# Keys of strided heads kept in order of time, and read with a step by the score products

## The chip, the cores and the metric

The kernel runs on one core of a Trainium2 chip. The metric is the device time of one execution in microseconds (us). The core's engines are TensorE (PE in the rows; PEld is its weight load), VectorE (DVE), ScalarE (ACT), GpSimd (POOL) and SyncE (SP), which issues the DMAs here.

## The reference

Three layers follow each other. The first is attention with 4 batches, 8 heads, 576 tokens and 64 values a head; four heads are local (a query sees the last 32 tokens), four are strided (a query sees the earlier tokens whose number has the same remainder by 32). The second is a layer with a softmax-weighted unit and a layer norm, the third a product of two projections.

```
scores = scale * np.matmul(q, k.transpose(0, 1, 3, 2))
mask_local = (rel >= 0) & (rel < stride)                                    # heads 0 to 3
mask_strided = (rel >= 0) & (pos[None, :] % stride == pos[:, None] % stride)   # heads 4 to 7
scores = np.where(masks, scores, -1e9);  attn = softmax(scores);  attn_out = attn @ v
h = x @ w_in;  solu = h * softmax(h);  ln = (solu - mu) / np.sqrt(var + 1e-06) * g_ln;  x = ln @ w_out
out = (x @ w_a) * (x @ w_b) @ w_out2
```

Inputs and outputs are float32; the weights arrive in 64-bit form and are converted in the kernel.

## The kernel before, in words

Attention works on pairs of heads: four pairs in each of four batches, two local and two strided. For each pair the queries and keys of 576 tokens are loaded in fp32 (rawq, rawk), transposed on TensorE into a PSUM tile s (line 594, six transposes each), and evacuated by ScalarE into qkT, queries in qkT[:, 0], keys in qkT[:, 1], so that the head dimension lies on partitions and the tokens along the free axis.

For a strided pair, two neighbouring tokens share a row of the load, so that partitions 0 to 63 hold the even tokens and 64 to 127 the odd ones. The columns that come out of the transpose are in order of time: for each head 18 periods t of 16 residues a. The evacuation (line 602) writes them by residue, h a t, so that the 18 tokens of a residue lie side by side: it reads PSUM in order and writes with a step of 18 fp32 words. For local pairs the evacuation is plain (line 605). The time that the planner is told for these is in line 606.

A strided tile (two for each pair, one for the even and one for the odd residues) covers 16 residues of two heads in twelve cells. A cell takes the queries of up to three residues, 54 columns, as the stationary operand and the keys of the same residues, 54 columns, as the moving one (lines 677 to 680); the cells of the sixth run have one residue, 18 columns. Before the cells a product of an identity with a mask fills the PSUM tile (line 676). In the trace each fp32 product is two records. Then follow the row maximum and softmax on VectorE and ScalarE (lines 692 to 710), the transposing of the probabilities (on TensorE in batch 0, line 739; by DMA afterwards, line 763), and the products with V (line 773 in batch 0, lines 778 to 780 afterwards), and ScalarE puts the output into xT (line 800). The layer after it takes tiles of 128 tokens (line 831, matmuls with w_in; line 881, with w_out) and runs among the attention of later batches. The third layer follows (lines 1268 and 1333).

The order of all instructions is set by a planner. Each step tells its engine and how long it should take; the planner makes a list schedule of them, then 40 more with keys that are taken from the schedule backward and shifted at random (fixed seed), and keeps the shortest. A changed time of one step can therefore move instructions of every engine anywhere in the program. Loads and stores go through SyncE's queue in the planned order, and a load stands there until its buffer is free.

Of the kernel before, what the change touches and what calls it, by code (L numbers as in the profile page):

```python
# [19 lines left out]
B, H, S, D = 4, 8, 576, 64  # L20
# [6 lines left out]
NR = S // ST  # L27
RP = ST // 2
# [222 lines left out]
def tile_banded_attention_solu_bilinear(  # L251
# [13 lines left out]
    nc = tc.nc  # L265
# [5 lines left out]
    def pe(us, fn, r, w, cols=60): return P.op("PE", us, fn, r, w, cols)  # L271
    def dve(us, fn, r, w): return P.op("DVE", us, fn, r, w)
    def act(us, fn, r, w): return P.op("ACT", us, fn, r, w)
# [253 lines left out]
    for b in range(B):  # L527
        for pr in range(H // 2):
            g = groups[b][pr] = Group()
# [55 lines left out]
    def group_T(g):  # L585
        g.T = rings["qkT"].new()
        for c in range(2):
            tp = rings["s"].new()
            raw = g.raw[c]

            def transposes(tp=tp, raw=raw):
                for m in range(NM):
                    i, o = divmod(m, NM // 2)
                    nc.tensor.transpose(tp()[:, i, QT * o:QT * o + QT], raw()[:, m].rearrange("p h d -> p (h d)"),  # L594
                                        ident[:QT, :QT])
            pe(NM * 0.085, transposes, ((raw, 0), (raw, 1), "ident"), (tp,), NM * 72)

            def evac(c=c, tp=tp):
                src = tp()[:, :, :S // 2]
                dst, sc = g.T()[:, c], 1.0 if c else D ** -0.5  # L600
                if g.strided:
                    nc.scalar.activation(dst.rearrange("p (h a t) -> p h t a", h=2, t=NR),  # L602
                                         src.rearrange("p h (t a) -> p h t a", t=NR), AF.Copy, scale=sc)
                else:
                    nc.scalar.activation(dst.rearrange("p (i t) -> p i t", i=2), src, AF.Copy, scale=sc)
            act(1.2 if g.strided else 0.66, evac, (tp,), ((g.T, c),))

    def vdims(g):
        return (128, len(RUNS) * 2 * D) if g.strided else (KB, NB * 2 * D)
# [31 lines left out]
    def att_tile(g, j, fine):  # L641
# [28 lines left out]
        def scores():  # L670
            s = sp()
            last = {(c[1], c[3]): n for n, c in enumerate(cells)}
            for f in banks:
                for rows, stop in ([(slice(0, 128), False)] if len(last) == 2 * len(banks) else
                                   [(slice(64 * x, 64 * x + 64), (f, x) not in last) for x in range(2)]):
                    nc.tensor.matmul(s[rows, f, :npb * nk], identb[:, rows], mask[:, :npb], start=True, stop=stop)  # L676
            for n, (h, f, col, half, _, nq, q0, kk, k0, *_) in enumerate(cells):
                w = slice(64 * f, 64 * f + 64)
                nc.tensor.matmul(s[64 * half:64 * half + nq, f, col:col + kk], g.T()[w, 0, q0:q0 + nq],  # L679
                                 g.T()[w, 1, k0:k0 + kk], start=False, stop=n == last[f, half])  # L680
        pe(ng * nk * 0.42e-3 + sum(0.04 if c[3] else 4 * c[7] / 2.4e3 for c in cells) + 0.03, scores,
           ((g.T, 0), (g.T, 1), "identb", "masks" if g.strided else "maskl"), (sp,),
           ng * nk + sum(c[7] for c in cells))
# [103 lines left out]
        t0 = g.b * S % XR  # L787
# [153 lines left out]
    def attention(b):  # L941
        P.sooner = pm["sooner"]
        gs = order[4 * b:4 * b + 4]
        ts = batch_tiles(b)
        P.key = pm["att"] * b - pm["pre"]
        for p in (gs[:2], gs[2:]):
            for g in p:
                load_v(g)
            if b not in pm["direct"]:
                pair_scale(p)  # L950
        for n, (g, j) in enumerate(ts):
            P.key = pm["att"] * (b + n / len(ts))
            if not j:
                P.key -= pm["pre"]
                group_T(g)
                if b not in pm["direct"]:
                    group_v(g)
                load_next()
                P.key += pm["pre"]
            att_tile(g, j, (b * len(ts) + n) in pm["fine"])  # L960
        P.sooner = 0.0
# [402 lines left out]
    for ps in range(NP):  # L1364
        for i in range(NSB):
            n = (i + ps) % NSB
# [67 lines left out]
```

## Time and profile before

| | |
|---|---|
| median of three timed runs | 757.65 us (756.41 to 758.9) |
| profiled execution | 755.28 us |
| its span, first to last instruction | 752.9 us |
| TensorE busy | 727.9 us, 97% |
| mean granted TensorE clock | 0.983 of full speed |

The span is cut by the profile into work of the engines and idle time; each idle stretch is put down to the event that ended it. A busy TensorE counts records from start to end, and records overlap, so how long a group of products takes is best read from the start of one group to the start of the next. The granted clock is 1.00 at 2.4 GHz and 0.5 at 1.2 GHz; a value between them is a stretch with both.

### The profile page before, as it was taken

What the parts mean: (1) busy time and instruction counts of PE and PEld (TensorE: products, weight loads), DVE (VectorE), ACT (ScalarE), POOL (GpSimd) and SP (SyncE); (2) the same over time, 40 slices, a digit from 0 to 9 for tenths busy, and PEclk for the clock granted to TensorE, in tenths of its full rate; (3) what the DMA queues carried; (4) which work ended last, traced back from release to release, by engine and by line L of the source; (5) the groups of instructions that cost most, each with busy time, mean ns of one, the idle gap of its engine ahead of it and who ended that gap; (6) DMA issues with size and microseconds to landing.
All of it is one profiled execution on the core that took longest, in us unless ns stands there. A gap on an engine that the chain in (4) does not pass through costs nothing.

```text
span 752.9 us, 14306 instructions
## 1 busy us (share of the span) xinstructions
PE 727.9 (97%) x5564; PEld 484.5 (64%) x5564; DVE 524.6 (70%) x1020; ACT 430.2 (57%) x800; POOL 119.9 (16%) x194
## 2 busy tenths in 40 slices
PE   6989899999999998989999999999999999999997
PEld 4867677878787786877645655556555545555553
DVE  5799988857757775898799998737777463435253
ACT  4568887676677677885666766537263433133130
POOL 4352436232513432210000000000000000000000
PEclk9989799999999999999999999999999999999999
DMA  9779997979874864976536234315614131720405
GB/s 209 187 174 234 195 177 164 255 148 190 146 132 91 184 138 93 246 184 240 169 118 244 66 112 141 113 57 175 221 43 129 57 104 40 228 85 30 139 1 167
DMA packets 156963, 109.59 MB, mean 146 GB/s; under 512 B 101344, under 2 KB 135136, under 8 KB 156896
## 3 DMA queue, kind: packets, MB, share of 16 engines
q1 hardware_dynamic: 156896, 108.69, 56.1%
q8 instruction: 43, 0.70, 0.4%
q14 instruction: 24, 0.20, 0.1%
HBM read 65.41 MB, written 27.53 MB: 123 GB/s over the span
## 4 chain that ended last, share of the span: by engine, by line
PE 90%; DVE 5%; ACT 2%; DMA 1%; issue 1%; POOL 0%; POOLq 0%; SPq 0%; DVEq 0%; ACTq 0%
PE M L1268 32%; PE o L1333 18%; PE h L831 14%; PE y L881 12%; PE s L679 4%; PE s L594 3%; PE xbank L778 2%; PE xbank L773 1%; PE s L676 1%; PE xbank L780 1%; PE xbank L779 1%; ACT qkT L602 1%; DMA rawk<-in_k_dram 1%; DMA lnT<-ln 1%; PE Q L897 0%
## 5 line engine op out<-in xcount | busy, mean ns | idle before, releaser
L1268 PE MATMUL M<-y,w 128*128 128x384 f16 x1512 | 258.1, 326 | 1.4 <-DVE y L1215 1.3
L1268 PEld LDWEIGHTS <-w 128*128 128x128 f16 x1512 | 147.0, 98 | 101.8 <-issue 2.1
L1333 PE MATMUL o<-wo,p 128*128 128x512 f16 x648 | 148.4, 379 | 0.2 <-DVE p L1320 0.2
L1333 PEld LDWEIGHTS <-p 128*128 128x128 f16 x648 | 63.1, 98 | 71.1 <-DVE p L1320 0.7
L881 PE MATMUL y<-lnT,wout 128*128 128x256 f16 x864 | 102.7, 274 | 3.0 <-ACT ys L884 1.9
L881 PEld LDWEIGHTS <-wout 128*128 128x128 f16 x864 | 82.7, 98 | 17.4 <-issue 4.8
L831 PE MATMUL h<-win,xh 128*128 128x512 f32 x288 | 81.1, 423 | 0.7 <-DVE wk L840 0.6
L1275 ACT COPY M<-M 128x384 f32<-128x384 f32 x72 | 33.6, 467 | 57.8 <-PE M L1268 57.6
L831 PEld LDWEIGHTS h<-win,xh 128*128 128x128 f32 x288 | 55.4, 200 | 12.6 <-DVE wk L840 1.0
L1318 ACT ACTIVATE p<-A 128x384 f16<-128x384 f32 x72 | 36.9, 522 | 37.3 <-DVE A L1317 37.0
L1340 DVE SCALAR_TENSOR_TENSOR ob<-o,osc,op 128x512 f32<-128x512 f32 x36 | 27.0, 749 | 41.0 <-PE o L1333 31.3
L1279 DVE TENSOR_TENSOR A<-M,V 128x384 f32<-128x384 f32 x36 | 19.8, 555 | 40.3 <-PE M L1268 40.3
L1290 ACT COPY V<-M 128x384 f32<-128x384 f32 x36 | 17.2, 477 | 46.7 <-PE M L1268 46.5
L1320 DVE SCALAR_TENSOR_TENSOR p<-A,p 128x384 f16<-128x384 f32 x72 | 39.0, 552 | 6.1 <-ACT p L1318 5.1
L831 PE MATMUL h<-win,xl 128*128 128x512 f32 x144 | 41.5, 412 | 0.0
L679 PE MATMUL s<-qkT 64*54 64x54 f32 (+2 forms) x672 | 38.7, 257 | 2.7 <-ACT qkT L602 2.7
L445 DVE SCALAR_TENSOR_TENSOR f64f<-f64f,raw 128x512 int32<-128x512 int32 x52 | 39.2, 758 | 1.8 <-ACT f64f L438 1.1
L438 ACT ACTIVATE f64f<-raw 128x512 f32<-128x512 f32 x52 | 34.1, 667 | 6.0 <-DMA raw<-in_moe_w_b_dram 3.7
L1317 DVE TENSOR_TENSOR A<-A,M 128x384 f32<-128x384 f32 x36 | 19.9, 552 | 24.5 <-PE M L1268 24.4
L679 PEld LDWEIGHTS s<-qkT 64*54 64x54 f32 (+2 forms) x672 | 28.1, 146 | 13.4 <-issue 4.6
L692 DVE TENSOR_REDUCE mx<-s 128x6 f32<-128x324 f32 (+2 forms) x40 | 19.2, 485 | 20.8 <-PE s L679 20.8
L861 DVE SCALAR_TENSOR_TENSOR ln<-wk,st,ln 128x1024 f16<-128x1024 f32 x18 | 24.4, 1358 | 13.0 <-ACT ln L860 13.0
(170 smaller groups left out, 1156.9 us busy)
## 6 DMA issues: line engine op xcount, KB each, us to landing
raw<-in_moe_w_out_dram SPq DMA_DIRECT2D x20, 512.0 KB
o_scr<-ob SPq DMA_DIRECT2D x36, 256.0 KB
op<-o_scr SPq DMA_DIRECT2D x36, 256.0 KB
raw<-in_moe_w_a_dram SPq DMA_DIRECT2D x12, 512.0 KB
raw<-in_moe_w_b_dram SPq DMA_DIRECT2D x12, 512.0 KB
y_scr<-y SPq DMA_DIRECT2D x14, 384.0 KB
y<-y_scr SPq DMA_DIRECT2D x14, 384.0 KB
y_scr<-ys SPq DMA_DIRECT2D x18, 256.0 KB
```

The costliest lines, as they stand in the source:

```text
L438: act(0.67, lambda: nc.scalar.activation(f(), raw()[:, :, 1].bitcast(F32), AF.Copy, scale=2.0 ** -112), (raw,), (f,))
L445: nc.vector.scalar_tensor_tensor(fi, fi, 3, raw()[:, :, 0], op0=ALU.logical_shift_left, op1=ALU.bitwise_or)
L679: nc.tensor.matmul(s[64 * half:64 * half + nq, f, col:col + kk], g.T()[w, 0, q0:q0 + nq], g.T()[w, 1, k0:k0 + kk], start=False, stop=n == ...
L831: nc.tensor.matmul(h()[:, 512 * n:512 * n + 512], xs[xa]()[:, kk], win[wa][:, kk, 512 * n:512 * n + 512], start=(pi == 0 and kk == 0), sto ...
L861: dve(1.29, lambda: nc.vector.scalar_tensor_tensor(ln()[:, 1], e(), st()[:, 7:8], ln()[:, 0], op0=ALU.mult, op1=ALU.subtract), (e, (st, 7) ...
L881: nc.tensor.matmul(y()[:, 256 * mi:256 * mi + 256], wout[:, kk, wa, 128 * m:128 * m + 128], lnT()[:, xa, kk], start=(pi == 0 and kk == 0), ...
L1268: nc.tensor.matmul(bank()[:, :HB], w()[:, wa, a, kk], y7[b]()[:, xa, kk], start=first and pi == 0 and kk == 0, stop=pi == 2 and kk == 1, s ...
L1275: act(TA, lambda: nc.scalar.copy(dst()[:, :HB], src()[:, :HB]), (src,), (dst,))
L1318: act(TA, lambda x=x, v=v: nc.scalar.activation(v(0), x(), AF.Copy, scale=2.0 ** -PEXP), (x,), ((pu, 0, c, t),))
L1320: dve(TD, lambda x=x, v=v: nc.vector.scalar_tensor_tensor(v(1), x(), 2.0 ** -PEXP, v(0), op0=ALU.mult, op1=ALU.subtract), (x, (pu, 0, c, t ...
L1333: nc.tensor.matmul(o(), pus[u]()[:, xa, c, 128 * tt:128 * tt + 128], wo()[:, 2 * u + c, wa], start=(u == 0 and c == 0 and pi == 0), stop=( ...
L1340: dve(0.75, lambda: nc.vector.scalar_tensor_tensor(ob(), o(), osc()[:, tt:tt + 1], op(), op0=ALU.mult, op1=ALU.add), (o, osc, op), (ob,))
```

## The change

Only the queries of a strided pair are still written by residue. Its keys are evacuated as those of local pairs are, in order of time, and the score products pick a residue's keys with an access pattern: up to three residues, one word apart, by 18 periods, 16 words (64 bytes) apart. The planner is told 0.66 us for this evacuation instead of 1.2 us. Queries, masks, probabilities and V keep their layout, and the columns of a cell come in the same order as before.

```diff
             def evac(c=c, tp=tp):
                 src = tp()[:, :, :S // 2]
                 dst, sc = g.T()[:, c], 1.0 if c else D ** -0.5
-                if g.strided:
+                if g.strided and not c:
                     nc.scalar.activation(dst.rearrange("p (h a t) -> p h t a", h=2, t=NR),
                                          src.rearrange("p h (t a) -> p h t a", t=NR), AF.Copy, scale=sc)
                 else:
                     nc.scalar.activation(dst.rearrange("p (i t) -> p i t", i=2), src, AF.Copy, scale=sc)
-            act(1.2 if g.strided else 0.66, evac, (tp,), ((g.T, c),))
+            act(1.2 if g.strided and not c else 0.66, evac, (tp,), ((g.T, c),))
...
+            def tokens(c, f, t0, n):
+                t = g.T()[64 * f:64 * f + 64, c]
+                if not (g.strided and c):
+                    return t[:, t0:t0 + n]
+
+                h, a = divmod(t0 // NR, RP)
+                return t[:, S // 2 * h:S // 2 * h + S // 2].rearrange("p (t a) -> p a t", a=RP)[:, a:a + n // NR]
             for n, (h, f, col, half, _, nq, q0, kk, k0, *_) in enumerate(cells):
-                w = slice(64 * f, 64 * f + 64)
-                nc.tensor.matmul(s[64 * half:64 * half + nq, f, col:col + kk], g.T()[w, 0, q0:q0 + nq],
-                                 g.T()[w, 1, k0:k0 + kk], start=False, stop=n == last[f, half])
+                nc.tensor.matmul(s[64 * half:64 * half + nq, f, col:col + kk], tokens(0, f, q0, nq), tokens(1, f, k0, kk),
+                                 start=False, stop=n == last[f, half])
```

From line 686 on, a line has a number higher by 7 than before; the score products of line 679 are those of line 686.

SyncE's queue before, from the last load of the second strided pair's keys on (raws_109 is the buffer of V of the first strided pair, a raw with a number a piece of weights):

```order
L544 DMA rawk<-in_k_dram 96x6x128
L561 DMA raws_109<-in_v_dram 18x6x128
L561 DMA raws_109<-in_v_dram 18x5x128
L550 DMA rawq<-in_q_dram 96x6x64 x2
L550 DMA rawk<-in_k_dram 96x6x64 x2
L433 DMA raw_239<-in_moe_w_in_dram 128x1024
L561 DMA raws_109<-in_v_dram 18x6x128
L561 DMA raws_109<-in_v_dram 18x5x128 x3
L433 DMA raw_276<-in_moe_w_in_dram 128x1024
L433 DMA raw_287<-in_moe_w_in_dram 128x1024
L550 DMA rawq<-in_q_dram 96x6x64 x2
```

The same queue from the same load on after the change:

```order
L544 DMA rawk<-in_k_dram 96x6x128
L433 DMA raw_176<-in_moe_w_in_dram 128x1024
L550 DMA rawq<-in_q_dram 96x6x64 x2
L550 DMA rawk<-in_k_dram 96x6x64
L561 DMA raws_109<-in_v_dram 18x6x128
L550 DMA rawk<-in_k_dram 96x6x64
L433 DMA raw_256<-in_moe_w_in_dram 128x1024
L550 DMA rawq<-in_q_dram 96x6x64
L561 DMA raws_109<-in_v_dram 18x5x128 x3
L561 DMA raws_109<-in_v_dram 18x6x128
L561 DMA raws_109<-in_v_dram 18x5x128
L433 DMA raw_318<-in_moe_w_in_dram 128x1024
```

The first load of w_in now stands ahead of all loads of V, and a load of queries of the second local pair stands ahead of five of the first pair's six loads of V.

ScalarE before, from its first evacuation on (e is the probabilities before they are normed, sm their sums):

```order
L602 ACTIVATE qkT<-s 128x2x18x16 x2
L704 ACTIVATE e<-e 128x324
L709 ACTIVATE sm_253<-sm_253 128x6
L602 ACTIVATE qkT<-s 128x2x18x16
L704 ACTIVATE e<-e 128x324
L438 ACTIVATE f64f<-raw_239 128x512
L602 ACTIVATE qkT<-s 128x2x18x16
```

The same engine from the same place on after the change:

```order
L602 ACTIVATE qkT<-s 128x2x18x16
L605 ACTIVATE qkT<-s 128x576
L438 ACTIVATE f64f<-raw_176 128x512
L711 ACTIVATE e<-e 128x324
L602 ACTIVATE qkT<-s 128x2x18x16
L716 ACTIVATE sm_262<-sm_262 128x6
L711 ACTIVATE e<-e 128x324
L466 CAST win_106<-f64f 128x512
L605 ACTIVATE qkT<-s 128x576
```

The keys' evacuations are those of line 605 now, and the first conversion of w_in stands ahead of the first exponential.

TensorE before, from the fourth score tile on (line 739 transposes probabilities, line 773 is the product with V):

```order
L679 MATMUL s<-qkT 54x54 x8
L773 MATMUL xbank<-PT,raws_109 64x54
L773 MATMUL xbank<-PT,raws_109 64x18
L773 MATMUL xbank<-PT,raws_109 64x54
L773 MATMUL xbank<-PT,raws_109 64x18
L773 MATMUL xbank<-PT,raws_109 64x54 x8
L739 MATMUL y<-ident,lnT 128x128 x3
L594 MATMUL s<-ident,rawq 128x96 x6
```

TensorE from the same tile on after the change:

```order
L686 MATMUL s<-qkT 54x54 x8
L746 MATMUL y<-ident,lnT 128x128 x3
L780 MATMUL xbank<-PT,raws_109 64x54
L780 MATMUL xbank<-PT,raws_109 64x18
L780 MATMUL xbank<-PT,raws_109 64x54
L780 MATMUL xbank<-PT,raws_109 64x18
L780 MATMUL xbank<-PT,raws_109 64x54 x8
L594 MATMUL s<-ident,rawq 128x96 x6
```

The transposes of the second tile's probabilities have moved ahead of the first tile's products with V.

## Rows read from the trace of the kernel before

**Rows 1.** The page's first part: busy us, share of the span, instructions.

```profile
PE 727.9 (97%) x5564; PEld 484.5 (64%) x5564; DVE 524.6 (70%) x1020; ACT 430.2 (57%) x800; POOL 119.9 (16%) x194
```

**Rows 2.** Five stretches: length, busy us of each engine, granted clock, DMA share, GB/s.

```profile
0.00:50.00 50.00, 41.51 (x390) 32.31 (x390) 34.35 (x68) 27.09 (x53) 21.64 (x40) 0.99 0.86 190
50.00:100.00 50.00, 45.20 (x370) 34.21 (x369) 46.67 (x91) 43.03 (x86) 18.45 (x26) 0.84 0.94 204
100.00:300.00 200.00, 195.81 (x2169) 157.55 (x2170) 141.27 (x264) 143.46 (x258) 71.50 (x117) 0.99 0.75 156
300.00:400.00 100.00, 96.38 (x658) 68.14 (x655) 88.82 (x172) 70.28 (x118) 8.36 (x13) 0.98 0.63 191
400.00:753.00 353.00, 348.98 (x1987) 192.30 (x1984) 213.48 (x428) 146.37 (x289) 0.00 (x0) 1.00 0.35 112
```

**Rows 3.** Waits of TensorE: us in total, times, longest us.

```profile
PE s L679 <- ACT qkT L602: 2.7, 3, 1.6
```

**Rows 4.** TensorE in order of time: start, us, line, count, idle time before and releaser.

```profile
8.22 2.04 PE L679 MATMUL s<-qkT 64*54 64x54 f32 x24 [0.77 <-ACT qkT L602]
10.20 0.45 PE L676 MATMUL s<-masks,identb 128*128 128x324 bf16 x1
...
17.51 2.04 PE L679 MATMUL s<-qkT 64*54 64x54 f32 x24 [0.37 <-ACT qkT L602]
...
74.06 1.36 PE L679 MATMUL s<-qkT 64*54 64x54 f32 x24 [1.60 <-ACT qkT L602]
```

**Rows 5.** ScalarE's groups to 300 us: count, busy us, mean ns, idle before.

```profile
L602 ACT ACTIVATE qkT<-s 128x576 f32<-128x576 f32 x16 | 18.9, 1180 | 9.0 <-PE s L594 9.0
L605 ACT ACTIVATE qkT<-s 128x576 f32<-128x576 f32 x16 | 10.3, 651 | 5.3 <-PE s L594 5.3
```

**Rows 6.** TensorE's groups to 420 us, strided score products by shape.

```profile
L679 PE MATMUL s<-qkT 64*54 64x54 f32 x320 | 22.6, 247 | 2.7 <-ACT qkT L602 2.7
L679 PE MATMUL s<-qkT 64*18 64x18 f32 x64 | 7.1, 187 | 0.0
```

**Rows 7.** TensorE in order of time, a warm strided tile of batch 2.

```profile
142.21 1.36 PE L679 MATMUL s<-qkT 64*54 64x54 f32 x24
143.50 0.31 PE L676 MATMUL s<-masks,identb 128*128 128x324 bf16 x1
```

**Rows 8.** TensorE in order of time, matmuls of the second layer at two clocks.

```profile
52.06 3.71 PE L831 MATMUL h<-win,xh 128*128 128x512 f32 x8
55.61 1.10 PE L831 MATMUL h<-win,xl 128*128 128x512 f32 x4
...
137.76 1.98 PE L831 MATMUL h<-win,xh 128*128 128x512 f32 x8
139.57 1.07 PE L831 MATMUL h<-win,xl 128*128 128x512 f32 x4
```

**Rows 9.** Stretches of 4 us, columns as in Rows 2.

```profile
48.00:52.00 4.00, 2.48 (x28) 2.11 (x24) 3.90 (x10) 2.44 (x8) 1.36 (x1) 0.59 0.63 134
52.00:56.00 4.00, 4.00 (x13) 3.19 (x12) 3.63 (x7) 4.00 (x8) 3.44 (x3) 0.55 0.79 221
```

**Rows 10.** ScalarE's groups to 300 us, attention outputs of batch 0 by shape.

```profile
L800 ACT ACTIVATE xT<-xbank 128x288 f32<-128x288 f32 x4 | 2.8, 688 | 5.0 <-PE xbank L773 5.0
...
L800 ACT ACTIVATE xT<-xbank 128x256 f32<-128x256 f32 x4 | 1.5, 372 | 0.0
...
L800 ACT ACTIVATE xT<-xbank 128x64 f32<-128x64 f32 x2 | 0.4, 214 | 0.0
```

**Rows 11.** SyncE's queue in order of time: start, us of issuing, line, count.

```profile
2.81 0.97 SPq L561 DMA_DIRECT2D raws<-in_v_dram  x2
...
9.00 1.47 SPq L561 DMA_DIRECT2D raws<-in_v_dram  x4
...
13.81 0.88 SPq L550 DMA_DIRECT2D rawq<-in_q_dram  x2
```

**Rows 12.** TensorE in order of time, the first product with V.

```profile
21.35 0.35 PE L773 MATMUL xbank<-PT,raws 54*64 54x54 f32 x1
```

## The prediction

> **What bounds the kernel now.** I read the share of each engine first. TensorE is busy for 97% of the span; no other engine is above 70% [rows 1]. By stretches the picture is sharper [rows 2]: TensorE stands idle 8.5 us in the first 50 us, 4.8 us in the next 50, 4.2 us in the 200 us after that, and 3.6 and 4.0 us in the rest. From 100 to 300 us, where most of the attention of batches 1 to 3 runs beside the second layer's matmuls, it is 98% busy, so there any nanosecond added to TensorE's stream lengthens the run and any taken off ScalarE alone gives nothing. Only in the first 100 us does another engine end waits of TensorE often enough to matter.
>
> The next view is the time that TensorE waits, by what ends it. For an evacuation of transposed queries or keys of a strided pair it waits 2.7 us before score products, in three places [rows 3]: 0.77 us at 8.22, 0.37 us at 17.51 and 1.60 us at 74.06 [rows 4]. Each time the evacuation that ends the wait is that of the keys: the transposes of rawk come last before it.
>
> **The evacuations.** Eight groups (two strided pairs in each of four batches) evacuate queries and keys. The strided form takes 1180 ns each, sixteen times; the plain form for the same 576 columns takes 651 ns [rows 5]. The change turns the eight of the keys into the plain form: 8 x 0.53 = 4.2 us less on ScalarE. Of that only what lies ahead of a waiting TensorE counts: at most 0.53 us in each of the three waits, so 0.53 + 0.37 + 0.53 = 1.4 us. The other five are hidden behind matmuls already, as no wait stands there. The ends for this term are 0 (whatever conversion stands next on ScalarE takes the place) and 4.2 us (all eight count). I take 1.4 us, because the waits are rows, not a guess.
>
> **The score products.** Nothing is added in number: a strided tile still issues 12 products in 24 records, and in a tile 20 records have 54 key columns and 4 have 18: 320 and 64 in sixteen tiles [rows 6]. What changes is how the keys are read: before, 54 neighbouring fp32 words; now three runs of 18 words, each word 64 bytes from the next. No row of the trace shows TensorE reading a stepped moving operand, so this is bounded from both sides.
>
> First, what a record costs now. Between two mask products the 24 records of a warm tile fill 142.21 to 143.50, that is 1.29 us or 54 ns each [rows 7]. In the first 20 us the same tile takes 8.22 to 10.20, 1.98 us or 82 ns each [rows 4]; the granted clock reads 1.00 there too, but the second layer's products that later take 226 ns (1.81 us for eight) take 464 ns (3.71 us for eight) in the stretch where it reads 0.55 [rows 8, 9], so I read the early tiles as run at the lower level, 1.2 GHz, too. Four tiles (batch 0) are of that kind, twelve are warm. That record also tells the rate at which TensorE takes an fp32 word: 512 columns in 226 ns, 0.44 ns a column, which is one column per cycle at 2.4 GHz. So 54 ns is about 22 ns of weight load, 22 ns of key columns and some 10 ns besides; it is a sum, since all products of a tile use the same 64 rows of the array. A slower key stream therefore adds to the record in full.
>
> Second, what a step does elsewhere in this kernel. ScalarE writes the stepped evacuation at 72 bytes from word to word. Against the plain form it loses (1180 - 651) / 576 = 0.92 ns a word. Its plain rate is (372 - 214) / (256 - 64) = 0.82 ns a word, from two unstepped outputs of line 800; the stepped output of the same line, 288 words 128 bytes apart, comes to (688 - 161) / 288 = 1.83 ns, with the 161 ns of fixed time that the two unstepped rows leave [rows 10]. So a step of this size halves the rate: 0.82 to 1.74 or 1.83 ns.
>
> The Trainium skill ("SBUF — State Buffer", section "SBUF: two separate sides") has a rule that speaks against the change: SBUF is read in lines of 16 bytes, and a stream that does not hit a line at least twice pays for each new one. With 64 bytes from word to word every key would be on a line of its own. The two ScalarE rows agree with it for writes; for a read by TensorE no row does, and the page gives no size.
>
> The ends are then these. Below: zero, if TensorE fetches ahead or reads each word in one go whatever its neighbours are; a gain is excluded, because the columns stay the same in number. Above: the whole stepped word time of ScalarE, 1.74 ns. A 54-column record would gain 54 x (1.74 - 0.42) = 71 ns, an 18-column record 24 ns; a warm tile 20 x 71 + 4 x 24 = 1.52 us, twelve of them 18.3 us; a tile at the lower level 54 x (1.74 - 0.83) = 49 ns in a record, 1.05 us a tile, four of them 4.2 us; in all 22.5 us. Between the ends I take the factor that the ScalarE rows show, not their time: a rate halved from 0.42 to 0.83 ns a word. A 54-column record gains 22.5 ns and an 18-column record 7.5 ns, a warm tile 20 x 22.5 + 4 x 7.5 = 0.48 us, twelve 5.8 us. At the lower level a column takes 0.83 ns already, so the four early tiles gain nothing. All twelve warm tiles lie in stretches where TensorE does not wait, with the exception of the one at 74.06, so I count the 5.8 us in full. What comes late behind a longer tile is the row maximum on VectorE, which waits for it, and behind that the softmax chain; TensorE has products of the second layer to run meanwhile, so I add nothing for these.
>
> **The order.** The planner is given 0.66 us in place of 1.2 us for eight evacuations and lays out the whole program anew, on all five engines. Two places deserve a price. On SyncE's queue the first load of w_in now stands ahead of all loads of V, and five of the six loads of the first pair's V stand behind a load of queries that must wait until the second pair's query transposes have freed the buffer; before, all six were ahead of it. That load was issued at 13.81 us and an issue takes 0.37 to 0.49 us, so the last of V is asked for by about 16.5 us, and the first product that reads it stood at 21.35 us [rows 11, 12]: almost 5 us to land. On ScalarE the first conversion of w_in now stands ahead of the first exponentials. If its data came late, the softmax of the first tile would stand behind it; the conversion is 0.67 us. On TensorE a block of probability transposes moves ahead of the first products with V, which gives those loads 0.8 us more. I charge nothing for the order and put 3.5 us to either side, about what the idle time of TensorE between 100 and 300 us could shrink or grow by.
>
> **Sum.** 5.8 - 1.4 = +4.4 us against the profiled execution, which took 755.28 us (a span of 752.9 us and 2.4 us around it): 759.7 us. That execution lies 2.4 us under the median of the three timed runs, 757.65 us, so on the scale of the median the forecast is 762 us.
>
> **Rivals.** (1) The step is free for TensorE. For it: the port takes one word per cycle of its own whatever the array does with it, and nothing in the trace shows TensorE's reads held up. Against it: ScalarE's rows. Only the gain is left: 757.65 - 1.4 = 756.2 us, with the order's 3.5 us to each side, so 752.7 to 759.7. This is the case that ends on the other side. (2) A new line costs TensorE the same time as it costs ScalarE, 1.74 ns a word, not the same factor. For it: if the time is that of the memory and not of the engine, this is what would be seen, and the Trainium skill's rule as worded would allow it. Against it: ScalarE pays for writes, and TensorE only reads. 757.65 + 22.5 - 1.4 = 778.7 us. (3) The order decides: the new layout meets a wait that the planner does not see, for instance the first exponentials behind a late w_in, or a different fall of the granted clock in 48 to 56 us, where it reads 0.59 and 0.55 [rows 9]. With a step that is free, one more 4 us stretch at the lower level in a TensorE-bound part would cost up to 2 us, so this would end near 759 to 761 us. It is a part of the spread of the other cases rather than a case with its own hardware cause.
>
> **How the numbers follow.** I give 0.42 to the forecast, 0.37 to a free step (the order's spread included) and 0.21 to the full word time. About 0.3% of this time, 2.3 us, is what a measurement of this kernel can tell from no change. Of the free case a bit over half is faster than 755.4, the rest mostly the same, a little slower: 0.19, 0.12, 0.06. Of the forecast's case 0.05 is faster and 0.08 the same, by the order's luck. The third is slower outright. That makes 0.24 faster, 0.20 the same and 0.56 slower. The forecast alone spans 758 to 766; the range that should hold 8 in 10 goes from 753, the low end of the free case, to 778, which takes in about half of the costly one.
>
> **What would show it.** The score tiles decide: a warm tile that still takes 1.29 us means a free step, about 1.8 us means halving, about 2.8 us the full word time. The eight evacuations of keys should read about 650 ns beside eight at 1180, and the waits of TensorE for them shrink from 2.7 to about 1.3 us. If the tiles are unchanged and the run is still slower, the order is the cause, and TensorE's idle time or its granted clock before 350 us must show it. If TensorE's busy time grows by 5 us and the span does not, then TensorE was not the bound I took it for.

## The result, and the profile after

The changed kernel took 764.98 us (median of six runs, 762.98 to 766.5) against 757.31 us for the kernel before in six runs beside them: a ratio of 1.0098, 95% interval 1.0077 to 1.0119, so 7.7 us slower. The forecast was 762 us and slower. Some executions of these kernels run in a slow state; all medians and ratios here are taken without them. The profiled execution of the changed kernel took 766.0 us, its span 764.1 us. Measured once more later, the ratio was 1.0131 (below).

The page's first part, after the change, answers to [rows 1]: busy us, share, instructions.

```profile
PE 739.9 (97%) x5564; PEld 491.2 (64%) x5564; DVE 520.4 (68%) x1020; ACT 427.2 (56%) x800; POOL 114.6 (15%) x194
```

TensorE is busy 12 us longer with the same 5564 matmuls, and ScalarE 3 us less. So the added time is work that takes longer on TensorE, not new waiting in sum: span less busy time is 25.0 us before and 24.2 us after. A part of it is seen in the strided tiles. TensorE of the changed kernel in order of time (start, us, line, count; the time of a tile is from its start to the start of what follows):

```profile
7.68 2.04 PE L686 MATMUL s<-qkT 64*54 64x54 f32 x24 [0.27 <-ACT qkT L605]
9.66 0.45 PE L676 MATMUL s<-masks,identb 128*128 128x324 bf16 x1
...
60.01 1.87 PE L686 MATMUL s<-qkT 64*54 64x54 f32 x24
61.81 0.64 PE L746 MATMUL y<-ident,lnT 128*96 128x128 f32 x4
...
74.52 1.86 PE L686 MATMUL s<-qkT 64*54 64x54 f32 x24 [1.02 <-ACT qkT L605]
76.31 0.45 PE L676 MATMUL s<-masks,identb 128*128 128x324 bf16 x1
76.69 2.04 PE L686 MATMUL s<-qkT 64*54 64x54 f32 x24
...
163.30 1.87 PE L686 MATMUL s<-qkT 64*54 64x54 f32 x24
165.10 0.37 PE L492 MATMUL xbank<-ident,am 128*2 128x128 f32 x1
165.27 0.48 PE L676 MATMUL s<-masks,identb 128*128 128x324 bf16 x1
165.67 2.05 PE L686 MATMUL s<-qkT 64*54 64x54 f32 x24
```

A warm tile takes 1.80 us (60.01 to 61.81, 163.30 to 165.10), where it took 1.29 us [rows 7]. An early tile at the lower clock takes 1.98 us, as before [rows 4]. Ten of the twelve later tiles are warm here; those at 76.69 and 165.67 take 1.97 and 1.98 us at the lower clock. In the kernel before, too, two of the twelve are not warm throughout: from 75.58 to the next product at 77.34 one takes 1.76 us, and one at 228.83 takes 1.63 us.

```profile
75.58 1.83 PE L679 MATMUL s<-qkT 64*54 64x54 f32 x24
```

Over all sixteen tiles, each from its start to the start of what follows, the two traces give 24.2 us before and 29.8 us after: 5.6 us. The evacuations (ScalarE's groups to 300 us) are as short as they should be, and the wait for them shrinks from 2.7 us [rows 3] to 1.3 in two places, 1.02 of it at 74.52 us:

```profile
L605 ACT ACTIVATE qkT<-s 128x576 f32<-128x576 f32 x24 | 15.3, 646 | 8.6 <-PE s L594 8.4
L602 ACT ACTIVATE qkT<-s 128x576 f32<-128x576 f32 x8 | 9.6, 1194 | 7.6 <-PE s L594 7.6
```

```profile
PE s L686 <- ACT qkT L605: 1.3, 2, 1.0
```

One thing more is new. In stretches of 4 us (length, busy us of each engine, granted clock, DMA share, GB/s) the changed kernel's clock falls for some 10 us behind 164 us:

```profile
160.00:164.00 4.00, 4.00 (x55) 2.83 (x54) 2.42 (x2) 3.45 (x5) 0.24 (x2) 1.00 0.75 139
164.00:168.00 4.00, 4.00 (x50) 2.90 (x48) 2.23 (x5) 0.78 (x1) 0.34 (x2) 0.58 0.82 160
168.00:172.00 4.00, 4.00 (x42) 3.32 (x41) 1.37 (x4) 2.03 (x3) 0.00 (x0) 0.50 0.21 69
172.00:176.00 4.00, 4.00 (x20) 3.02 (x19) 3.45 (x10) 2.56 (x6) 1.26 (x3) 0.64 0.48 148
```

The same stretches before read 1.00 throughout. TensorE is busy in all of them. From 60 to 400 us the mean granted clock of this execution is 0.95, against 0.97 before (the lines stand with e8 below): 340 x 0.02, an estimated 7 us of lost time. So the 12 us of added busy time are about half tiles and half clock. The second tile above, from 165.67 on, and the products with V after it run at 1.2 GHz.

So two suspects stood: the step (0.51 us in each warm tile, 6.1 us if all twelve were warm, 5.6 us as traced) and the order.

### The profile page after: what moved, and what is told of

It reads as the page before. It is cut to its first block, busy times and chain, and to the rows that moved or that the text cites. A ratio compares the mean times of both kernels' runs of the same rounds, so it can differ in the third digit from the quotient of the medians.

```text
span 764.1 us, 14315 instructions
## 1 busy us (share of the span) xinstructions
PE 739.9 (97%) x5564; PEld 491.2 (64%) x5564; DVE 520.4 (68%) x1020; ACT 427.2 (56%) x800; POOL 114.6 (15%) x194
## 4 chain that ended last, share of the span: by engine, by line
PE 53%; DVE 4%; ACT 1%; DMA 1%; issue 0%; POOL 0%; DVEq 0%; POOLq 0%; ACTq 0%
PE M L1275 31%; PE o L1340 18%; PE y L888 2%; PE h L838 1%; DVE y L1222 1%; DVE yst L1198 1%; DMA lnT<-ln 1%; PE Q L904 0%; PE Q L1205 0%; PE Q L1185 0%; DVE ln L868 0%; DVE w L1111 0%; DVE yst L1227 0%; DVE Z L1233 0%; DVE S L1097 0%
## 5 line engine op out<-in xcount | busy, mean ns | idle before, releaser
L838 PE MATMUL h<-win,xh 128*128 128x512 f32 x288 | 84.2, 433 | 0.6 <-DVE wk L847 0.5
L838 PEld LDWEIGHTS h<-win,xh 128*128 128x128 f32 x288 | 57.0, 207 | 13.1 <-DVE wk L847 1.0
L686 PE MATMUL s<-qkT 64*54 64x54 f32 (+2 forms) x672 | 44.8, 273 | 1.3 <-ACT qkT L605 1.3
L445 DVE SCALAR_TENSOR_TENSOR f64f<-f64f,raw 128x512 int32<-128x512 int32 x52 | 36.9, 715 | 7.9 <-ACT f64f L438 7.5
L686 PEld LDWEIGHTS s<-qkT 64*54 64x54 f32 (+2 forms) x672 | 31.3, 149 | 14.1 <-issue 4.0
L761 POOL TENSOR_TENSOR e<-e,r 128x324 f32<-128x324 f32 (+2 forms) x30 | 25.6, 857 | 55.1 <-DVE r L717 53.4
```

The source lines that it names most:

```text
L445: nc.vector.scalar_tensor_tensor(fi, fi, 3, raw()[:, :, 0], op0=ALU.logical_shift_left, op1=ALU.bitwise_or)
L761: pool(0.1 + 1.2 * pl, lambda: nc.gpsimd.tensor_tensor(ev(), ev(), r()[:, :ng].unsqueeze(2).to_broadcast([128, ng, nk]), op=ALU.mult), (r, ...
L838: nc.tensor.matmul(h()[:, 512 * n:512 * n + 512], xs[xa]()[:, kk], win[wa][:, kk, 512 * n:512 * n + 512], start=(pi == 0 and kk == 0), sto ...
```

## The experiments

They form a table of two questions: which order the planner laid out, and how the keys are read. The kernels e5 to e7 were run once each, for the time of a tile; all others were run six or more times, with runs of the kernel before on the same chip.

**The order alone.** The kernel before, with one number changed:

```diff
-            act(1.2 if g.strided else 0.66, evac, (tp,), ((g.T, c),))
+            act(1.2 if g.strided and not c else 0.66, evac, (tp,), ((g.T, c),))
```

> The layout of keys and the score products as before the change; only the planner is told 0.66 us for the evacuation of strided keys, so that all instructions stand in the order of the changed kernel. Theory (the step costs 0.5 us in each of twelve warm tiles, and the new order costs the rest): warm tiles take 1.29 us, the eight evacuations of keys 1180 ns, and the median lies 2 to 5 us over before (7.7 us of the change less 6.0 for the step, plus 1.4 for the slower evacuations); the granted clock falls to 0.5 for some 10 us near 165 to 175 us, as it does in the changed kernel. Rival (the step costs all of it, by its tiles and by a fall of the clock that the slower tiles bring about): no fall of the clock there, and the median within 1.5 us of before.

Measured: 1.0076 (1.0052 to 1.0099), 761.87 against 755.22 us, 6.6 us between the medians. Warm tiles take 1.29 us. The clock does fall near 166 us, for about 7 us. So the fall belongs to the order and not to the step, and the order costs more than expected; the rival is out.

**The access alone.** The changed kernel, but the planner is told the old 1.2 us, so that every instruction stands where it stood before:

```diff
-            act(1.2 if g.strided and not c else 0.66, evac, (tp,), ((g.T, c),))
+            act(1.2 if g.strided else 0.66, evac, (tp,), ((g.T, c),))
```

> The changed kernel's evacuation of keys and stepped score products, in the order of the kernel before (the planner is told 1.2 us as before). Theory: warm strided tiles take 1.80 us instead of 1.29, tiles at the lower clock stay at 1.98 us, and the median lies 4 to 5 us over before (12 x 0.51 = 6.1 less 1.4 for the evacuations). Rival (the step costs all 7.7 us): 6.5 to 8 us over before, with one more stretch of a lower granted clock than before.

Measured: 1.0052 (1.0024 to 1.0081), 759.64 against 755.22 us: 4.4 us, as the theory has it. A warm tile, TensorE in order of time:

```profile
145.66 1.87 PE L686 MATMUL s<-qkT 64*54 64x54 f32 x24
147.46 0.31 PE L676 MATMUL s<-masks,identb 128*128 128x324 bf16 x1
```

1.80 us. So about half of the loss is the stepped read, less what the shorter evacuations give back, and it does not need the new order.

**The step taken out again.** From here on to e7 the access alone is the base, in the order of before, and only the keys that a product reads differ:

```diff
-                return t[:, S // 2 * h:S // 2 * h + S // 2].rearrange("p (t a) -> p a t", a=RP)[:, a:a + n // NR]
+                return t[:, t0:t0 + n]
```

> As the access alone in the order of before, but the score products read as many neighbouring key columns instead of stepped ones (the keys of other tokens, so the values are other ones). Theory: warm tiles are back at 1.29 us, and what is left is the gain of eight plain evacuations: 1 to 1.5 us under before. Rival (the gain of the evacuations is taken by the next conversion on ScalarE): within 0.5 us of before.

Measured: 0.9986 (0.9958 to 1.0014), 753.42 us; the tile is back.

```profile
140.38 1.36 PE L686 MATMUL s<-qkT 64*54 64x54 f32 x24
141.67 0.31 PE L676 MATMUL s<-masks,identb 128*128 128x324 bf16 x1
```

The gain of the evacuations, 1.8 us between medians and 1.1 us by the ratio, is of the size expected, but the interval holds zero, so it isn't shown. Between this kernel and the access alone, on one chip, lie 6.2 us between medians and 5.0 us by the ratios, and only the step differs: over their sixteen tiles the two traces have 24.4 and 29.8 us, 5.4 us apart.

The profiles show a second difference. Stretch 88 to 108 us (columns as in the stretches above), first this kernel, then the access alone in its two profiled executions (e2, and e10 below):

```profile
88.00:108.00 20.00, 18.30 (x249) 13.62 (x250) 17.64 (x34) 16.90 (x31) 7.15 (x10) 0.91 0.96 186
88.00:108.00 20.00, 17.78 (x206) 12.64 (x205) 15.98 (x33) 15.32 (x28) 7.60 (x11) 0.74 1.00 186
88.00:108.00 20.00, 17.88 (x174) 12.86 (x172) 13.64 (x29) 13.22 (x24) 6.78 (x10) 0.57 0.82 170
```

The clock stays at the lower level longer where the keys are read with the full step: 0.74 and 0.57 against 0.91, which is also what the kernel before has there. That is the second sign that was named for the rival, a longer lower clock, though the time fits the theory. Both profiled executions of the access alone (763.45 and 766.75 us) lie above their medians, 759.64 and 759.81 us, so a usual execution loses less this way. How much of the step's cost comes through the clock is not separated.

**What the step costs by its length.** Three words side by side, then a jump of 64 bytes:

```diff
-...rearrange("p (t a) -> p a t", a=RP)[:, a:a + n // NR]
+...rearrange("p (t a) -> p t a", a=RP)[:, :, a:a + n // NR]
```

> As the access alone in the order of before, but the three residues of a cell are the inner dimension: three neighbouring words, then 64 bytes on (the columns of a cell come in another order than mask and values have, so the values are other ones). Theory (a word that does not share its line of 16 bytes with its neighbour costs a second step of the read): the rate lies between, with about 1.4 to 1.6 us a warm tile, and 0 to 2 us over before. Rival (any pattern that is not one run is read at half rate): 1.80 us a tile and 4 to 5 us over before. Second rival (the mean rate of three words in a period is enough to hide it): 1.29 us and 1 us under before.

```profile
140.50 1.45 PE L686 MATMUL s<-qkT 64*54 64x54 f32 x24
141.88 0.31 PE L676 MATMUL s<-masks,identb 128*128 128x324 bf16 x1
```

Measured: 0.9997 (0.9974 to 1.0019), a tile of 1.38 us. That is 0.09 us over a plain one, a little under the expected range, and far from the half rate of the rival; the time cannot tell the theory from a free step, the tile can. Then constant steps of w = 2, 3 and 4 words:

```diff
-                return t[:, S // 2 * h:S // 2 * h + S // 2].rearrange("p (t a) -> p a t", a=RP)[:, a:a + n // NR]
+                t0 = min(t0, S - w * n)
+                return t[:, t0:t0 + w * n].rearrange("p (t a) -> p a t", a=w)[:, 0]
```

> The access alone in the order of before, but with a step of 2 words (8 bytes) instead of 16, so each line of 16 bytes holds two of the words read (keys of other tokens, so the values are other ones). Theory (a word that is the only one read of its line of 16 bytes takes one more cycle, 0.42 ns): no such word, a warm tile takes 1.29 us. Rival (any step halves the rate): 1.80 us.

```profile
139.21 1.38 PE L687 MATMUL s<-qkT 64*54 64x54 f32 x24
140.52 0.31 PE L676 MATMUL s<-masks,identb 128*128 128x324 bf16 x1
```

> As with a step of 2 words, but 3 words (12 bytes): of four words that follow each other two share a line and two stand alone (other keys are read, so the values are other ones). Theory (one more cycle for each word alone in its line): 27 of 54 words and 9 of 18 pay 0.42 ns, 20 x 11.3 + 4 x 3.8 = 0.24 us a tile, 1.53 us. Rival (the step alone decides, with its limit at 16 bytes): 1.29 us.

```profile
139.25 1.65 PE L687 MATMUL s<-qkT 64*54 64x54 f32 x24
140.83 0.31 PE L676 MATMUL s<-masks,identb 128*128 128x324 bf16 x1
```

> As with a step of 2 words, but 4 words (16 bytes): every word is alone in its line (other keys are read, so the values are other ones). Theory: the same 1.80 us a warm tile as with 16 words. Rival (the cost grows with the distance): between 1.29 and 1.80 us.

```profile
147.23 1.91 PE L687 MATMUL s<-qkT 64*54 64x54 f32 x24
149.07 0.31 PE L676 MATMUL s<-masks,identb 128*128 128x324 bf16 x1
```

By the step in bytes, a warm tile takes 1.29 us at 4, 1.31 at 8, 1.58 at 12, 1.84 at 16 and 1.80 at 64. So neither "any step" nor "the distance" is what counts. A tile reads 20 x 54 + 4 x 18 = 1152 words; 0.51 us over that is 0.44 ns a word, one cycle at 2.4 GHz (0.42 ns) for each word, where every word is alone on its 16 bytes. At 12 bytes two of four words are alone: 0.24 us expected, 0.29 measured. In the runs of three, if a period of 16 words starts on a line, the run of words 3 to 5 and that of words 6 to 8 each leave one word alone: 18 words in each of eight records, and all 18 of the four short records, 216 words or 0.09 us, which is what was measured. I had not counted that before the run. The last 0.04 us between 16 and 64 bytes has no explanation here. The single times of these three were 752.33, 753.97 and 765.0 us against a median of 754.55 us for before. The last is 10.5 us over; its tiles explain 6.2 us of that (30.3 against 24.2 us over all sixteen), and its granted clock in the stretch from 88 to 108 us is 0.74, as in e2.

**The order with plain reads.** The changed kernel in its own order, with the plain read of e3:

```diff
-                return t[:, S // 2 * h:S // 2 * h + S // 2].rearrange("p (t a) -> p a t", a=RP)[:, a:a + n // NR]
+                return t[:, t0:t0 + n]
```

> The changed kernel in its own order, with plain evacuations of the keys, but with score products that read neighbouring columns (keys of other tokens, so the values are other ones). Theory (the order costs about 3 us of its own, the step about 5): warm tiles at 1.29 us and the median 2 to 4.5 us over before. Rival (the order is harmless once the evacuations are as short as the planner believes): within 1 us of before, and no stretch of a lower granted clock near 165 us.

Measured: 1.0079 (1.0052 to 1.0107), 760.8 against 754.55 us. More than expected: the order costs 6 us even where nothing is stepped and the evacuations are as short as the planner was told. Beside e3, which is the same work in the old order, one can see where. First e3's stretches, then those of e8:

```profile
60.00:100.00 40.00, 36.45 (x355) 27.53 (x356) 36.65 (x75) 36.44 (x73) 15.28 (x23) 0.87 1.00 212
100.00:140.00 40.00, 38.97 (x423) 31.47 (x424) 34.04 (x65) 29.66 (x54) 16.72 (x23) 1.00 0.83 187
140.00:200.00 60.00, 59.38 (x706) 47.60 (x699) 42.52 (x78) 42.15 (x79) 20.94 (x35) 1.00 0.84 181
```

```profile
60.00:100.00 40.00, 33.79 (x247) 25.25 (x245) 33.97 (x68) 32.57 (x66) 10.07 (x19) 0.83 0.91 188
100.00:140.00 40.00, 37.67 (x517) 30.44 (x517) 33.43 (x70) 27.70 (x55) 15.43 (x22) 1.00 0.91 166
140.00:200.00 60.00, 60.00 (x601) 47.86 (x599) 38.19 (x66) 40.47 (x70) 21.64 (x34) 0.94 0.88 200
```

TensorE (the first busy time) loses 2.7 us to waiting in 60 to 100 us and 1.3 us in the next 40, and from 140 to 200 it is busy throughout but at 0.94 of the clock. One of the waits can be followed. ScalarE of e3 and of e8 before and after the evacuation of keys (line 605) that a strided tile waits for:

```profile
70.53 1.05 ACT L852 ACTIVATE ln<-wk 128x1024 f32<-128x1024 f32 x1
71.49 0.19 ACT L852 ACTIVATION_READ_ACCUMULATOR ln<-wk 128x1 f32 x1
71.58 0.62 ACT L605 ACTIVATE qkT<-s 128x576 f32<-128x576 f32 x1
72.11 0.66 ACT L438 ACTIVATE f64f<-raw 128x512 f32<-128x512 f32 x1
```

```profile
71.23 0.60 ACT L827 CAST xh<-xT 128x512 fp32r<-128x512 f32 x1
72.45 0.70 ACT L438 ACTIVATE f64f<-raw 128x512 f32<-128x512 f32 x1 [0.62 <-DMA raw<-in_moe_w_out_dram]
73.03 0.66 ACT L605 ACTIVATE qkT<-s 128x576 f32<-128x576 f32 x1
```

In the old order the evacuation goes first and the conversion of w_out after it; in the new one the conversion stands ahead and waits 0.62 us for its data, with the evacuation behind it. TensorE of e8 pays:

```profile
70.63 0.31 PE L676 MATMUL s<-masks,identb 128*128 128x324 bf16 x1
73.74 2.04 PE L686 MATMUL s<-qkT 64*54 64x54 f32 x24 [2.80 <-ACT qkT L605]
75.71 0.45 PE L676 MATMUL s<-masks,identb 128*128 128x324 bf16 x1
```

It waits 2.80 us there, in e3 1.43 us. How much of the order's cost is waiting can be read from the stretch 60 to 400 us, in turn of before, e1, e3, e8, the changed kernel and e2:

```profile
60.00:400.00 340.00, 328.48 (x3154) 252.91 (x3155) 267.29 (x509) 249.41 (x445) 93.77 (x150) 0.97 0.74 172
60.00:400.00 340.00, 324.54 (x3136) 252.09 (x3135) 262.72 (x503) 248.11 (x443) 88.71 (x150) 0.97 0.74 172
60.00:400.00 340.00, 328.58 (x3131) 252.81 (x3132) 265.75 (x508) 247.71 (x445) 93.45 (x150) 0.97 0.72 171
60.00:400.00 340.00, 324.12 (x3104) 250.78 (x3103) 260.36 (x500) 243.70 (x439) 89.22 (x150) 0.96 0.75 169
60.00:400.00 340.00, 328.23 (x3106) 254.09 (x3106) 256.27 (x492) 240.69 (x434) 88.45 (x150) 0.95 0.73 169
60.00:400.00 340.00, 329.43 (x3093) 254.26 (x3092) 257.69 (x490) 242.13 (x435) 92.50 (x150) 0.95 0.70 164
```

TensorE stands idle 11.5 us before and 15.5 in e1, 11.4 in e3 and 15.9 in e8, at nearly the same clock. So with plain reads the order costs 4.0 to 4.5 us of waiting, and less through the clock. In the changed kernel, in the same order, TensorE stands idle 11.8 us, hardly more than before, and the clock is 0.95; but in e2, stepped in the old order, it is 0.95 as well, with 10.6 us idle. So in these executions a lower clock in sum goes with the step in either order, and the order's waiting hardly shows where the keys are read with the step. The wait above is one of several; I have not traced the rest one by one, nor the cause of the fall of the clock near 165 us, which came in all three kernels profiled in this order (the changed one, e1, e8) and not in that of before or e3.

**Do the two add up?** The changed kernel and the access alone once more, on one chip:

> The changed kernel once more, beside the access alone in the order of before on the same chip. Theory (step and order add up): 1.2 to 1.4% over before, since the order with plain reads was 0.8% and the step, as access alone less plain read, 0.66%. Rival (in the order of the changed kernel the step costs less, since part of it falls where TensorE waits or runs at the lower clock): 0.9 to 1.1%.

> The access alone in the order of before, once more. Theory: 0.5 to 0.65% over before, so that the changed kernel's order costs another 0.6 to 0.8% on top. Rival: 0.3 to 0.4% under the changed kernel.

Measured: 1.0131 (1.0102 to 1.016) for the changed kernel and 1.0069 (1.004 to 1.0098) for the access alone. The difference, 0.6%, is the order, close to e1's and e8's 0.8%. That fits a sum better than e10's rival (0.3 to 0.4% between the two). The rival of e9 is not out: the first measurement of the changed kernel, 0.98%, lies in its range and under the theory's, and the intervals of the two measurements overlap (up to 1.0119 and from 1.0102), so whether the step costs a little less in the new order stays open.

**Was the new order an unlucky draw?** The kernel before with other seeds for the planner's random shifts:

```diff
-PARAM = dict(early=(0,), seed=0, ...
+PARAM = dict(early=(0,), seed=1, ...      (and seed=2)
```

> The kernel before with another seed for the planner's random shifts, so another order with the same work. Theory (the order of before is a favourable draw, and another draw of the same planner costs as much as the changed kernel's order): 0.4 to 1% over before. Rival (the changed order is an unlucky draw): within 0.3% of before.

> The kernel before with a third seed, for the same question. Theory: 0.4 to 1% over before. Rival: within 0.3% of before.

Measured: 1.0049 (1.002 to 1.0079) and 1.0072 (1.0043 to 1.0101). Both are slower, with the same work and the same access. So the order of before looks like the lucky one: each of three other orders costs 0.5 to 0.8% (3.7 and 6.2 us between the medians for these two, 6.6 for e1). Three draws are few, and the changed kernel itself was not laid out with other seeds, so whether a better order exists for it is untested.

No version beat the kernel before by more than its interval. The plain read of e3, at 0.9986, reads the keys of other tokens, and the runs of three, at 0.9997, would need masks and V in another order as well.

## Why the prediction was right, and where it was not

- **The bound.** TensorE was taken as the bound, so that a longer score tile counts in full. It does, as far as the noise lets one say: 5.0 to 6.2 us between e2 and e3, whose tiles differ by 5.4 us.
- **The step.** It was bounded from 0 to 22.5 us and put at half the rate, 5.8 us, by the factor of ScalarE's stepped writes [rows 5, 10]. Measured: 1.80 us a warm tile where about 1.8 was named, 0.51 us more where 0.48 was worked out. That all twelve later tiles are warm was a misreading. Two of them were partly at the lower clock even in the kernel before (1.76 us at 75.58, 1.63 us at 228.83). All sixteen tiles grew by 5.6 us from trace to trace, near the 5.8 forecast. That the four early tiles would gain nothing, since at the lower clock a column takes 0.83 ns already, came out as well. The split of a record into weight load and key columns has no row of its own; what the runs show is that the longer key stream is paid in full. The 464 ns of a product at the lower clock are the length of a group; from start to start [rows 8] it is 444 ns, and nothing hangs on it. Both rivals on the hardware are out: the step isn't free, and a word alone costs TensorE 0.4 ns more, not ScalarE's time. The Trainium skill's rule ("SBUF — State Buffer", section "SBUF: two separate sides") that a line of 16 bytes wants two hits agrees with the five steps measured, and with the runs of three; the page has no size for it, and here it is 0.44 ns a word.
- **The evacuations.** 646 ns, and waits down to 1.3 us, as forecast. The gain of 1.4 us fits what e3 shows (1.1 us by the ratio, 1.8 between medians), but stays within the interval.
- **The order: the step that failed.** "I charge nothing for the order and put 3.5 us to either side." It costs 0.6 to 0.8%, some 5 to 6 us, more than the 3.5 us that were allowed for it. The two places that were given a price did no harm: the first product with V starts at 21.82 us in the changed kernel with no wait before it, and the early conversion of w_in delays nothing that TensorE waits for (the first tile starts at 7.68 instead of 8.22). What costs was elsewhere. With plain reads it is 4.0 to 4.5 us more waiting of TensorE from 60 to 400 us, of which one wait was followed, behind a conversion of w_out at 72 us. In the changed kernel the same conversion stands there too, but TensorE waits only 1.02 us, against 1.60 us before [rows 4], and in sum it waits no longer. Its clock falls near 165 us, but e2 has as low a mean from 60 to 400 us without that fall. So where the order's cost sits with plain reads is known in part, and where it sits in the changed kernel stays open; that it is there is shown by the medians alone (e9 against e10). The sign that was named for a costly order with unchanged tiles, idle time or granted clock before 350 us, did show in e1 and e8. The error was to treat a new layout as equally likely to gain and to lose: three other orders all lost.
- **The sum.** +4.4 us forecast, +7.7 measured: the step 5 to 6 (5.8 forecast), the evacuations an estimated -1.1 to -1.8, not shown clear of noise (-1.4), the order the rest, some 3 to 4 us in the first measurement and more in the later ones (0 forecast). The rival that the order decides came true as an addition, not in place of the step. The first measurement lies in the span of 758 to 766 us that the forecast alone was given; the later one, 1.31%, over the same 757.65 us would be 767.6 us, and lies only in the wider range that was kept for the other cases.

## What to carry to other kernels

Where a matmul's moving fp32 operand is picked from a longer row, look at how many of the words that it reads share 16 bytes with another: words alone run at half the rate at full clock, and runs of three neighbours cost little (0.09 us a tile here). Here reordering once, while evacuating on an engine with time to spare, was cheaper than reading with a step on the engine that bounds the kernel. And when a planner with random shifts lays out a program, a changed time of one step is a new draw: measure the order alone and the change in the old order, or the two can't be told apart.

## What the runs showed of the hardware

A moving fp32 word that is the only one read of its 16 bytes costs TensorE 0.44 ns more at 2.4 GHz (1.80 against 1.29 us for 1152 words), and nothing at 1.2 GHz (1.98 us both ways: the early tiles, and, where the granted clock reads 0.50, 1.97 us for the plain tile of e8 at 73.74 and 1.98 us for the stepped one of the changed kernel at 165.67). A step of 8 bytes costs 0.02 us a tile, 12 bytes 0.29, 16 bytes 0.55 and 64 bytes 0.51, at 2.4 GHz.
